# One product scales both heads of a query tile in the first attention, with the inverse sums in a PSUM bank

## The chip, the cores and the metric

The kernel runs on one core of a Trainium2 chip. The metric is device microseconds of one launch. The core has five queues of instructions that run side by side and wait for each other through semaphores: TensorE (PE) multiplies matrices into PSUM, VectorE (DVE) and ScalarE (ACT) work elementwise on SBUF and PSUM, GpSimd (POOL) works elementwise on SBUF, and SyncE (SP) issues DMAs. Within a queue the order is fixed when the program is built.

## The reference

Four batches, eight heads, 768 positions, 64 values a head. Attention sees the 96 positions behind a query (its own included) and the first 8 positions, with a bias that falls with distance. What comes out is the input of a mixture of four two-layer experts.

```python
scores = scale * np.matmul(q, k.transpose(0, 1, 3, 2)) + bias
scores = np.where(keep, scores, -1e9)
scores = scores - scores.max(-1, keepdims=True)
a = np.exp(scores)
a = a / (a.sum(-1, keepdims=True) + 1e-09)
x = np.matmul(a, v)                      # to (B*S, H*D) = (3072, 512)
for e in range(4):
    out += p[:, e:e+1] * (np.maximum(x @ w1[e], 0) @ w2[e])
```

## The kernel before, in words

**The first attention.** Batch 0 must have its attention output `x` before the experts have anything to multiply, so the launch begins with `attention_early`. It takes the heads in four pairs (0, 2, 1, 3), and each pair in six query tiles of 128 rows: 24 tiles in all. A tile's scores lie in windows of 256 columns per head (128 for the first tile of a pair). The local function `flow` drives a pipeline in which four tiles are in work at once. One call of `flow` does, in this order:

- `scores_early` for the newest tile and its neighbour (PE, in every second call);
- `softmax(one, two)`: for each head of tile *one*, DVE adds the bias and takes the minimum (`nmax`), and ACT takes the exponential and its row sum (`zsum`). Between them, DVE finishes tile *two*: it adds 1e-9 to `zsum`, takes the reciprocal, and scales the two heads of `pb` with one `tensor_scalar` each;
- `turn(three)`: PE transposes the scaled tile *three* into `pt`, and ACT copies it to `pT`;
- `weigh`, in every third call: PE multiplies the `pT` of three finished tiles by `v` into the bank `px` (20 matrix passes where the first tile of a pair is among them, 24 otherwise), and ACT copies 384 columns of `px` to `x`.

In a call with `weigh`, the three tiles were turned in earlier calls; tile *two* of that call, which DVE scales at the same time, is not among them.

So there are eight weighs: tiles 0 to 2 and tiles 3 to 5 of each pair. They are called the first to the eighth weigh below. The first falls into the call in which tile 4 of the pair is scaled, the second into the call in which tile 1 of the next pair is scaled, and so on. At the eighth no tile is left to scale.

**What sets the order.** While `Ordered.on` is set, each engine keeps the order in which the program is written. Waits are put in by the language's tile layer: an instruction that touches a tile waits for the last instructions of other engines that touched the same tile, whichever columns each of them used. All eight PSUM banks are taken in this stage: four by the scores, three by `pt`, one by `px`.

**Beside and behind it.** Between the calls of `flow`, POOL and SP prepare the first expert weights, and `first_sums` and `opening` start on the first expert as soon as half of `x` is there. Behind the attention PE works through the experts of batch 0, and the attention of the other batches is spread over the experts' work by `attention_chain`, which calls the same `softmax` and `weigh` with `early=False`.

The elementwise helper that records each instruction is line 43, so most rows of the profile carry L43; tiles are told apart by their names.

Of the kernel before, what the change touches and what calls it, by code (L numbers as in the profile page):

```python
# [9 lines left out]
F32 = mybir.dt.float32  # L10
# [3 lines left out]
AF = mybir.ActivationFunctionType  # L14
ALU = mybir.AluOpType
# [3 lines left out]
P = 128  # L19
# [167 lines left out]
def attn_moe_kernel(ctx: ExitStack, tc, q, k, v, n_global, n_local, domain_probs, w1, w2, out):  # L187
# [9 lines left out]
    HALF = S // 2  # L197
# [12 lines left out]
    ve, ac, po, sy, te = (Ordered(tc, e) for e in (nc.vector, nc.scalar, nc.gpsimd, nc.sync, nc.tensor))  # L210
# [173 lines left out]
    def windows(A, vt):  # L384

        vg = A.vg.tile([P, 2, NQT, D], F32, name="vg")
        sy.dma_start(vg[:NPREV], vt[NGLOB:])
        po.tensor_copy(vg[NPREV:], vt[:NGLOB, :, 0:1, :].to_broadcast([NGLOB, 2, NQT, D]))
        return vg
# [17 lines left out]
    def scores_early(A, t0, got):  # L407


        heads = [A.ps.tile([P, 2, 2 * P], F32, name=f"ps{j}") for j in range(2)]  # L410
        for t in (t0, t0 + 1):
            c0 = max(t - 1, 0) * PL + (0 if t == 0 else NGLOB)
            n = P if t == 0 else 2 * P
            for j in range(2):
                own = slice(j * D, (j + 1) * D)
                win = got["k"].rearrange("p t c -> p (t c)")[own, c0 : c0 + n]
                te.matmul(heads[j][:, t - t0, :n], got["q"][own, t, :], win, start=True, stop=True)
        return [[heads[j][:, i] for j in range(2)] for i in range(2)]

    def softmax(A, new, old):  # L420


        if old:
            pb, zsum = old["pb"], old["zsum"]
        if new:
            t, pr, ps = new["t"], new["pr"], new["ps"]
            cols = slice(0, P) if t == 0 else slice(0, 2 * P)
            bcol = slice(2 * P, 3 * P) if t == 0 else slice(0, 2 * P)
            new["pcol"] = pcol = slice(P, 2 * P) if t == 0 else slice(0, 2 * P)
            nmax = A.small.tile([P, 2], F32, name="nmax")  # L430
            new["zsum"] = A.small.tile([P, 2], F32, name="zsum")
            new["pb"] = A.pb.tile([P, 2, 2 * P], F32, name="pb")
        for j in range(2):
            if new:
                e = new["pb"][:, j, pcol]
                ve.tensor_tensor_reduce(
                    e, ps[j][:, cols], nbias[:, 2 * pr + j, bcol], 1.0, 3.0e38, ALU.add, ALU.min, nmax[:, j : j + 1]
                )
                ac.activation(
                    e, e, AF.Exp, bias=nmax[:, j : j + 1], scale=-1.0, accum_out=new["zsum"][:, j : j + 1]  # L440
                )
            if old:
                if j == 1:
                    ve.reciprocal(zsum, zsum)
                elif A.early:

                    old["spare"] = spare = A.small.tile([P, 3], F32, name="spare")
                    ve.tensor_scalar(zsum, zsum, 1e-9, None, op0=ALU.add, op1=ALU.add, accum_out=spare[:, 2:3])
                else:
                    ac.activation(zsum, zsum, AF.Copy, bias=1e-9)  # L450
        if old:
            for j in range(2):
                p = pb[:, j, old["pcol"]]
                if A.early:
                    ve.tensor_scalar(
                        p, p, zsum[:, j : j + 1], None, op0=ALU.mult, op1=ALU.add, accum_out=old["spare"][:, j : j + 1]
                    )
                else:
                    ac.activation(p, p, AF.Copy, scale=zsum[:, j : j + 1])

    def turn(A, tile_):

        t, pb = tile_["t"], tile_["pb"]
        pt = A.pt.tile([P, 2, 2, P], F32, name="pt")
        pT = A.pT.tile([P, 2, 2, P], F32, name="pT")
        w0 = 1 if t == 0 else 0
        for w in range(w0, 2):
            for j in range(2):
                te.transpose(pt[:, w, j, :], pb[:, j, w * P : (w + 1) * P], ident)
        ac.copy(pT[:, w0:], pt[:, w0:])  # L470
        tile_["pT"] = pT

    def weigh(A, three, x, b):

        px = A.px.tile([P, 512], F32, name=A.pxname)
        for i, tile_ in enumerate(three):
            t, pr, pT = tile_["t"], tile_["pr"], tile_["pT"]
            vt, vg = tile_["v"]["v"], tile_["v"]["vg"]
            for w in range(1 if t == 0 else 0, 2):
                for j in range(2):  # L480
                    vv = vt[:, j, t] if w == 1 else vg[:, j, t - 1]
                    te.matmul(
                        px[j * D : (j + 1) * D, i * P : (i + 1) * P],
                        vv,
                        pT[:, w, j, :],
                        start=(w == 1 if t == 0 else w == 0),
                        stop=(w == 1),
                    )
        cols = slice((t - TPH + 1) * P, (t + 1) * P)
        if x is not None:  # L490
            ac.copy(x[:, pr, cols], px[:, :HALF])
        else:
            piece = A.st.tile([P, HALF], F32, name="piece")
            ac.copy(piece, px[:, :HALF])
            ac.dma_start(xd[b][:, pr, cols], piece)
# [3 lines left out]
    def attention_early(A):  # L499

        b = 0
        x = xs[b] = xp.tile([P, NPAIR, S], F32, name="x")
        tiles, turned, ahead = [None] * 4, [], [None]

        def flow(new=None):

            one, two, three, four = tiles
            if new:
                if new["t"] % 2 == 0:
                    new["ps"], ahead[0] = scores_early(A, new["t"], gots[new["pr"]])  # L510
                else:
                    new["ps"] = ahead[0]
            if four:
                turned.append(four)
            softmax(A, one, two)
            if three:
                turn(A, three)
            if len(turned) == TPH:
                weigh(A, turned, x, b)
                turned.clear()  # L520
            tiles[:] = [new, one, two, three]

        def start(pr):

            nats[pr] = {n: next(load(A, src, b, pr, n)) for n, src in (("q", q), ("k", k), ("v", v))}

        def prepare_all(pr):

            nat, got = nats[pr], gots[pr]
            got["v"] = nat  # L530
            prepare_early(A, nat["q"], 0, "q", got)
            if pr:
                yield 1
            prepare_early(A, nat["k"], 0, "k", got)
            yield 1
            nat["vg"] = windows(A, nat["v"])
            prepare_early(A, nat["k"], 1, "k", got)
            yield 1
            prepare_early(A, nat["q"], 1, "q", got)
            yield 1  # L540

        nats, gots = {}, [{} for _ in range(NPAIR)]
        halves = [load(A, src, b, 0, n, 2) for n, src in (("q", q), ("k", k))]
        bias = biases(start_stack.enter_context(tc.tile_pool(name="setup", bufs=1)))
        next(bias)
        nats[0] = dict(zip(("q", "k"), (next(h) for h in halves)))
        for h in halves:
            next(h)
        nats[0]["v"] = next(load(A, v, b, 0, "v"))
        todo = [prepare_all(pr) for pr in PAIRS]  # L550
        next(bias)
        next(todo[0])
        start(PAIRS[1])
        for m, pr in enumerate(PAIRS):
            cur = gots[pr]
            for t in range(NQT):
                if t == 2 and m + 2 < NPAIR:
                    start(PAIRS[m + 2])
                flow({"t": t, "pr": pr, **cur})
                if (m, t) in BIASES:  # L560
                    next(bias)
                for _ in range(AHEAD[m][t]):
                    while todo and next(todo[0], 0) == 0:
                        todo.pop(0)
                yield
        while any(tiles):
            flow()
            yield
# [401 lines left out]
    with ExitStack() as start_stack:  # L970
        A = Pools(start_stack, "start", st=1, kd=2, qd=2, nat=2, natv=3, pb=4, ps=2, pt=3, px=1, early=True)
# [11 lines left out]
    op = main.enter_context(tc.tile_pool(name="op", bufs=1))  # L983
# [3 lines left out]
    A = Pools(  # L987
        att_stack, "att", st=1, kd=1, qd=2, nat=1, natv=1, pb=2, ps=2, pt=2, px=0, early=False, side="right"
    )
# [463 lines left out]
```

## Time and profile before

| what | value |
|---|---|
| median of 3 runs | 1165.45 us (1165.42 to 1165.84) |
| the profiled execution's own time | 1164.69 us |
| its span | 1162.9 us |
| PE busy | 1140.5 us, 98% |
| DVE busy | 853.2 us, 73% |
| ACT busy | 618.2 us, 53% |
| POOL busy | 606.6 us, 52% |

PE is the engine of the whole launch. The first 60 us, which hold the first attention, are another kind of stage: the four engines PE, ACT, DVE and POOL hand tiles to each other, and which of them is last changes on the way. The chain of waits (the profile's view of what ended last, followed back) and the timelines of single engines show that.

### The profile page before, as it was taken

To read this page: it belongs to the slowest core of one execution; us is meant where nothing else is said; L and a number is where in the kernel's file an instruction comes from. 1 tells how busy PE (TensorE), PEld (TensorE's weight loads), DVE (VectorE), ACT (ScalarE), POOL (GpSimd) and SP (SyncE) were. 2 spreads that over 40 slices of the span, in tenths; PEclk is the share of its full clock that TensorE was granted. 3 is DMA by queue.
4 is the path that set the end of the run, shared out by engine and by line. 5 is a ranking of instruction groups with operands and counts; after the bars stand their busy time and mean duration, and the time that the engine had idled before them with its cause. 6 is when DMAs were issued, how large, how long until landed. Compare 5 with 4: busy or idle time off the path is not lost.

```text
span 1162.9 us, 21146 instructions
## 1 busy us (share of the span) xinstructions
PE 1140.5 (98%) x7474; PEld 1062.6 (91%) x7474; DVE 853.2 (73%) x1944; ACT 618.2 (53%) x1597; POOL 606.6 (52%) x592
## 2 busy tenths in 40 slices
PE   7899999999999999999999999999999999999997
PEld 5678898989888989899998899999999999999997
DVE  7977776767767777776776777777777777777776
ACT  6854767777653665655565334444445444444443
POOL 5676645554343314222222327777778855555554
PEclk9999999999999999999999999999999999999999
DMA  9558798778775889978868668888887687777764
GB/s 185 149 172 290 268 294 258 269 253 255 247 261 206 282 269 286 282 234 279 257 196 288 207 215 304 306 302 300 284 314 281 240 303 239 249 247 247 245 232 131
DMA packets 181744, 294.32 MB, mean 253 GB/s; under 512 B 86400, under 2 KB 137088, under 8 KB 169344
## 3 DMA queue, kind: packets, MB, share of 16 engines
q1 hardware_dynamic: 177600, 286.61, 75.0%
q10 hardware_dynamic: 4032, 6.30, 1.5%
q8 instruction: 61, 1.00, 0.4%
q14 instruction: 51, 0.42, 0.1%
HBM read 207.93 MB, written 70.78 MB: 240 GB/s over the span
## 4 chain that ended last, share of the span: by engine, by line
PE 87%; DVE 5%; ACT 3%; POOL 2%; DMA 1%; issue 1%; DVEq 0%; ACTq 0%; POOLq 0%
PE pm L43 36%; PE pf L43 19%; PE X L43 11%; PE Y L43 9%; PE pt L43 7%; PE ps L43 4%; ACT pb L43 1%; DVE pb L43 1%; POOL w1s L43 1%; PE px L43 1%; DVE acc L43 1%; DVE xB L43 1%; DMA x_last<-piece 0%; DVE hA L43 0%; DVE pm L43 0%
## 5 line engine op out<-in xcount | busy, mean ns | idle before, releaser
L43 PE MATMUL pm<-w2s,h 128*128 128x512 f32 x1152 | 282.8, 395 | 3.6 <-DVE h L43 2.6
L43 PEld LDWEIGHTS pm<-w2s,h 128*128 128x128 f32 x1152 | 210.7, 188 | 46.5 <-DVE h L43 4.5
L43 ACT ACTIVATE hf<-pf 128x384 f32<-128x384 f32 x128 | 62.8, 491 | 248.3 <-DVE pf L43 247.1
L43 POOL TENSOR_TENSOR hS<-sf,hS 128x384 fp32r<-128x384 f32 x126 | 134.3, 1084 | 113.0 <-ACT hS L43 112.2
L43 DVE SCALAR_TENSOR_TENSOR acc<-pm,prob,acc 128x512 f32<-128x512 f32 x180 | 132.4, 748 | 54.5 <-PE pm L43 53.6
L43 POOL TENSOR_TENSOR sums<-raw 128x256 f32<-128x256 f32 x54 | 39.2, 745 | 211.8 <-DMA raw<-in_moe_w_dram 133.4
L43 PE MATMUL pm<-xT,w1s 128*128 128x384 f32 x744 | 147.9, 341 | 0.0
L43 PE MATMUL pf<-xT,w1s 128*128 128x384 f32 x768 | 146.5, 335 | 0.9 <-ACT hf L43 0.7
L43 PEld LDWEIGHTS pf<-xT,w1s 128*128 128x128 f32 x768 | 131.4, 188 | 1.7 <-ACT hf L43 1.2
L43 PEld LDWEIGHTS pm<-xT,w1s 128*128 128x128 f32 x744 | 128.0, 188 | 0.7 <-issue 0.7
L43 ACT ACTIVATE pb<-pb,nmax 128x256 f32<-128x256 f32 (+1 forms) x192 | 94.2, 498 | 58.1 <-DVE nmax L43 54.2
L43 DVE TENSOR_TENSOR hA<-hf,hA 128x384 fp32r<-128x384 f32 x94 | 84.6, 925 | 50.6 <-ACT hA L43 49.1
L43 PE MATMUL pm<-xB,w1s 128*128 128x384 f32 x574 | 116.8, 344 | 0.1
L43 PE MATMUL pf<-xB,w1s 128*128 128x384 f32 x576 | 110.7, 335 | 0.2 <-ACT hf L43 0.2
L43 PEld LDWEIGHTS pm<-xB,w1s 128*128 128x128 f32 x574 | 99.9, 188 | 5.5 <-issue 1.4
L43 ACT ACTIVATE h<-pm 128x384 fp32r<-128x384 f32 x128 | 62.0, 490 | 74.4 <-DVE pm L43 73.3
L43 PEld LDWEIGHTS pf<-xB,w1s 128*128 128x128 f32 x576 | 98.7, 188 | 0.6 <-ACT hf L43 0.4
L43 POOL TENSOR_TENSOR sf<-hf 128x384 f32<-128x384 f32 x63 | 70.3, 1116 | 43.6 <-ACT hf L43 43.6
L43 DVE CUSTOM_DVE_ANT_0 pb<-ps,nbias 128x256 f32<-128x256 f32 (+1 forms) x192 | 72.3, 395 | 5.8 <-PE ps L43 4.8
L43 DVE SCALAR_TENSOR_TENSOR h<-pm,h 128x384 fp32r<-128x384 f32 x128 | 69.5, 550 | 8.4 <-ACT h L43 6.8
L43 PE MATMUL Y<-w2b,hS 128*128 128x256 f32 x576 | 74.0, 282 | 0.0
L43 PE MATMUL X<-w2b,hS 128*128 128x256 f32 x576 | 73.9, 282 | 0.0
(159 smaller groups left out, 2183.5 us busy)
## 6 DMA issues: line engine op xcount, KB each, us to landing
w1s<-kept SPq DMA_DIRECT2D x47, 1792.0 KB, 8.2
w2b<-kept SPq DMA_DIRECT2D x224, 256.0 KB, 4.3
kept<-w1s SPq DMA_DIRECT2D x16, 1792.0 KB, 7.3
raw<-in_moe_w_dram SPq DMA_DIRECT2D x43, 512.0 KB, 4.7
kept<-w2s SPq DMA_DIRECT2D x16, 1024.0 KB, 6.9
w2s<-kept SPq DMA_DIRECT2D x16, 1024.0 KB, 5.5
qd<-qd SPq DMA_DIRECT2D x48, 192.0 KB, 3.2
v<-in_v_dram SPq DMA_DIRECT2D x16, 384.0 KB, 4.1
```

Source lines behind the costliest of these rows:

```text
L43: ins = fn(*args, **kwargs)
```

## The change

In the first attention alone, the reciprocal of `zsum` is written to four spare columns of the bank that `weigh` uses for `px` (two columns for tiles of even number, two for odd). One DVE `tensor_tensor` then multiplies both heads of the tile by these two numbers, broadcast along the columns. The bank `A.bank` is one tile for the whole stage, where before each `weigh` took a fresh tile from a pool with one buffer. The later attentions are as before.

```diff
             if old:
-                if j == 1:
+                if j == 1 and A.early:
+                    inverse = A.inverse[:, old["t"] % 2]
+                    ve.reciprocal(inverse, zsum)
+                elif j == 1:
                     ve.reciprocal(zsum, zsum)
                 elif A.early:
-                    old["spare"] = spare = A.small.tile([P, 3], F32, name="spare")
-                    ve.tensor_scalar(zsum, zsum, 1e-9, None, op0=ALU.add, op1=ALU.add, accum_out=spare[:, 2:3])
+                    spare = A.small.tile([P, 1], F32, name="spare")
+                    ve.tensor_scalar(zsum, zsum, 1e-9, None, op0=ALU.add, op1=ALU.add, accum_out=spare)
...
-        if old:
+        if old and A.early:
+            p = pb[:, :, old["pcol"]]
+            ve.tensor_tensor(p, inverse.unsqueeze(2).to_broadcast(list(p.shape)), p, op=ALU.mult)
+        elif old:
             for j in range(2):
                 p = pb[:, j, old["pcol"]]
-                if A.early:
-                    ve.tensor_scalar(
-                        p, p, zsum[:, j : j + 1], None, op0=ALU.mult, op1=ALU.add, accum_out=old["spare"][:, j : j + 1]
-                    )
-                else:
-                    ac.activation(p, p, AF.Copy, scale=zsum[:, j : j + 1])
+                ac.activation(p, p, AF.Copy, scale=zsum[:, j : j + 1])
...
     def weigh(A, three, x, b):
-        px = A.px.tile([P, 512], F32, name=A.pxname)
+        px = A.bank[:, :HALF] if A.early else A.px.tile([P, 512], F32, name=A.pxname)
...
     def attention_early(A):
         x = xs[b] = xp.tile([P, NPAIR, S], F32, name="x")
+        A.bank = A.px.tile([P, 512], F32, name="px")
+        A.inverse = A.bank[:, HALF : HALF + 4].rearrange("p (t j) -> p t j", j=2)
```

How the instructions stand, with the semaphores each waits for. First DVE at the second weigh: the end of the call in which tile 1 of the second pair is scaled, and the next call. `ISA pb,nmax<-ps,nbias` is the bias and minimum of one head, `zsum` the row sums. Before:

```order
L43 RECIPROCAL zsum<-zsum 128x2 [waits DVE_49]
L43 TENSOR_SCALAR pb,spare<-pb,zsum 128x256 [waits DVE_49]
L43 TENSOR_SCALAR pb,spare<-pb,zsum 128x256
L43 ISA pb,nmax<-ps_415,nbias 128x256 [waits PE_49]
L43 ISA nmax 128x1
L43 TENSOR_SCALAR zsum,spare<-zsum 128x2 [waits Activation_49]
L43 ISA pb,nmax<-ps_416,nbias 128x256
L43 ISA nmax 128x1
L43 RECIPROCAL zsum<-zsum 128x2 [waits DVE_49]
```

The same place now:

```order
L43 RECIPROCAL px<-zsum 128x2 [waits DVE_49]
L43 TENSOR_TENSOR pb<-px,pb 128x512 [waits DVE_49]
L43 ISA pb,nmax<-ps_409,nbias 128x256 [waits PE_49]
L43 ISA nmax 128x1
L43 TENSOR_SCALAR zsum,spare<-zsum 128x2 [waits Activation_49]
L43 ISA pb,nmax<-ps_410,nbias 128x256
L43 ISA nmax 128x1
L43 RECIPROCAL px<-zsum 128x2 [waits DVE_49,Activation_49]
L43 TENSOR_TENSOR pb<-px,pb 128x512 [waits DVE_49]
```

Two scalings have become one product, and the reciprocal of the call behind the weigh now also waits for ACT, whose last access to the bank is the copy from `px` to `x`. The same wait stands behind each of the first seven weighs.

PE at the same weigh: `pt<-ident,pb` are the transposes of tile *three*, `px<-pT` the products of the weigh. Before:

```order
L43 MATMUL pt<-ident,pb 128x128 [waits DVE_49,Activation_49]
L43 MATMUL pt<-ident,pb 128x128 [waits DVE_49]
L43 MATMUL px<-pT,vg 64x128 x2
L43 MATMUL px<-pT,v 64x128 x2
L43 MATMUL px<-pT,vg 64x128 x2
```

And now:

```order
L43 MATMUL pt<-ident,pb 128x128 [waits DVE_49,Activation_49]
L43 MATMUL pt<-ident,pb 128x128
L43 MATMUL px<-pT,vg 64x128 [waits DVE_49]
L43 MATMUL px<-pT,vg 64x128
L43 MATMUL px<-pT,v 64x128 x2
```

The order is the same, but the first product of the weigh now waits for DVE: for the product that scales tile *two* of the same call, the last DVE instruction before it in the program that read the bank. This wait stands at the first seven weighs as well.

SP in the first attention, at the loads of the last pair:

```order
+L1426 TENSOR_LOAD flag [waits Pool_49]
+L1426 ISA x2
 L43 DMA v<-in_v_dram 128x12x64 [waits DMAHW3_49,PE_49,Pool_49]
 L43 DMA vg<-v 96x768 [waits DMAHW5_49,DMAHW4_49]
 L43 DMA w1s<-in_moe_w_dram 128x4x256
-L43 DMA raw_490<-in_moe_w_dram 128x2x512 [waits DMAHW6_49]
-L1423 TENSOR_LOAD flag [waits Pool_49]
-L1423 ISA x2
+L43 DMA raw_481<-in_moe_w_dram 128x2x512 [waits DMAHW6_49]
```

The read of the flag for the general path stands four DMAs earlier. Behind the first attention no engine's order differs.

## Rows read from the trace of the kernel before

**Rows 1.** Stretches: start:end, length, busy us (instructions) by engine, PEclk, DMA, GB/s.
```profile
20.00:41.00 21.00, 20.70 (x204) 15.79 (x203) 19.30 (x124) 21.00 (x73) 11.96 (x16) 1.00 0.69 178
41.00:62.00 21.00, 16.66 (x147) 11.56 (x148) 17.39 (x93) 14.52 (x45) 13.23 (x15) 1.00 0.39 107
...
75.00:100.00 25.00, 25.00 (x134) 23.15 (x132) 18.52 (x33) 11.88 (x24) 22.79 (x22) 1.00 0.96 323
```

**Rows 2.** Chain that ended last, first 61 us: start, length, engine, tile, instructions.
```profile
36.60 1.22 ACT pb L43 x4
...
51.66 1.22 DVE pb L43 x5
...
59.98 0.49 ACT x L43
```

**Rows 3.** DVE timeline, second weigh: start, length, instruction, idle before it and releaser.
```profile
25.01 0.15 DVE L43 TENSOR_SCALAR_CACHE_REDUCE zsum<-zsum 128x2 f32<-128x2 f32 x1 [0.26 <-ACT pb L43]
...
25.44 0.16 DVE L43 RECIPROCAL zsum<-zsum 128x2 f32<-128x2 f32 x1
25.63 0.48 DVE L43 TENSOR_SCALAR_CACHE_REDUCE pb<-pb,zsum 128x256 f32<-128x256 f32 x1
...
26.04 0.47 DVE L43 TENSOR_SCALAR_CACHE_REDUCE pb<-pb,zsum 128x256 f32<-128x256 f32 x1
```

**Rows 4.** PE timeline, second weigh: its first and last products, then next transposes.
```profile
24.73 0.44 PE L43 MATMUL px<-pT,vg 128*64 128x128 f32 x4
...
25.87 0.39 PE L43 MATMUL px<-pT,v 128*64 128x128 f32 x4
...
27.73 0.66 PE L43 MATMUL pt<-ident,pb 128*128 128x128 f32 x4
```

**Rows 5.** ACT timeline, second weigh: copy of `px`, next copy of `pT`.
```profile
26.92 0.54 ACT L43 COPY x<-px 128x384 f32<-128x384 f32 x1
...
28.66 0.65 ACT L43 COPY pT<-pt 128x512 f32<-128x512 f32 x1
```

**Rows 6.** DVE timeline, reciprocals at the first, fifth, sixth and seventh weigh.
```profile
19.75 0.16 DVE L43 RECIPROCAL zsum<-zsum 128x2 f32<-128x2 f32 x1
...
43.28 0.15 DVE L43 RECIPROCAL zsum<-zsum 128x2 f32<-128x2 f32 x1
...
45.23 0.16 DVE L43 RECIPROCAL zsum<-zsum 128x2 f32<-128x2 f32 x1
...
49.70 0.16 DVE L43 RECIPROCAL zsum<-zsum 128x2 f32<-128x2 f32 x1
...
51.47 0.16 DVE L43 RECIPROCAL zsum<-zsum 128x2 f32<-128x2 f32 x1
...
55.00 0.16 DVE L43 RECIPROCAL zsum<-zsum 128x2 f32<-128x2 f32 x1
```

**Rows 7.** ACT timeline, copies of `px` at the first, fifth and sixth weigh.
```profile
21.49 0.50 ACT L43 COPY x<-px 128x384 f32<-128x384 f32 x1
...
44.49 0.47 ACT L43 COPY x<-px 128x384 f32<-128x384 f32 x1
...
50.71 0.47 ACT L43 COPY x<-px 128x384 f32<-128x384 f32 x1
```

**Rows 8.** PE timeline, after a wait, and the seventh weigh's first products.
```profile
48.43 0.50 PE L43 MATMUL pt<-ident,pb 128*128 128x128 f32 x2 [1.51 <-DVE pb L43]
...
54.85 0.44 PE L43 MATMUL px<-pT,v 128*64 128x128 f32 x4
```

**Rows 9.** DVE timeline, products of 384 and of 768 columns.
```profile
64.51 0.96 DVE L43 TENSOR_TENSOR xB<-x,xB 128x768 fp32r<-128x768 f32 x1 [1.34 <-ACT xB L43]
...
67.59 0.56 DVE L43 TENSOR_TENSOR u<-pm,u 128x384 f32<-128x384 f32 x1
```

**Rows 10.** One tile's instructions: `acc` from PSUM, ns of one as min/median/max.
```profile
L43 DVE SCALAR_TENSOR_TENSOR acc<-pm,prob,acc x11: 740/750/751, 94.9 to 119.0; 128x512 f32<-128x512 f32 x11
```

**Rows 11.** POOL timeline: the first instruction behind the attention.
```profile
65.29 1.86 POOL L43 TENSOR_TENSOR xT<-xB,xT 128x768 fp32r<-128x768 f32 x1 [9.94 <-ACT xT L43]
```

## The prediction

> **What bounds the kernel now.** I read the page's busy shares first, then the stretches, then the chain of waits, then the timelines of DVE, PE and ACT around each weigh. PE is busy 98% of the span, and behind the first attention it has no gap: 25.00 of the 25 us from 75 to 100 [rows 1]. So whatever makes `x` of batch 0 later moves everything behind it, unless a gap takes it in. The first attention has two stages. From 20 to 41 us ACT is busy 21.00 of 21 us while DVE has 19.30 [rows 1], the chain there runs through ACT's exponentials, and DVE waits for them before it adds 1e-9 to the sums [rows 2, 3]. From 41 to 57 us the chain runs through DVE's `pb`, and it ends with ACT's copy of the eighth weigh at 59.98 [rows 2]. In both stages the engines are interlocked within one or two microseconds, so a new wait among PE, ACT and DVE counts more than a shorter instruction on one of them.
>
> **What is removed.** Each of 24 tiles loses two scalings. At the second weigh they start at 25.63 and 26.04, 0.41 us apart [rows 3], so two take 0.82 us from start to start. The add of 1e-9 and the reciprocal stay.
>
> **What is added: the product.** No row shows a product of 512 columns with a broadcast operand. A product of 384 columns with one operand in PSUM takes 0.56 us, and one of 768 columns 0.96 us [rows 9]; the slope, 0.40 us for 384 columns, gives 0.56 + 0.13 = 0.69 us for 512. The nearest row of 512 columns from PSUM, with three operands, takes 0.75 us [rows 10]. I take 0.70 us. The ends are 0.56 us (the 384-column row itself, if the broadcast side came free) and 0.75 us. The next DVE instruction starts about 0.07 us before an instruction's end (0.48 long, 0.41 to the next start, [rows 3]), so the product takes 0.63 us from start to start, and a tile gains 0.82 - 0.63 = 0.19 us of DVE. The four first tiles of a pair, at half the width, gain about as much.
>
> The Trainium skill, in "VectorE: DVE Perf Modes", section "The perf-mode tier table", says that fp32 `tensor_scalar` in SBUF runs at two elements a cycle, and fp32 `tensor_tensor` at one. By that rule the two scalings should cost half of what the product costs, and the merger would lose DVE time. The trace does not agree for these scalings, which write an accumulator: 0.41 us for 256 columns is no faster per column than the 384-column product. By the rule the sum below would be about 2 us higher; I go by the rows.
>
> **What is added: two waits in a ring.** At the first seven weighs, PE's first `px` product waits for the product of tile *two* of the same call, and the next call's reciprocal waits for ACT's copy of `px`. Before, neither waited: at the second weigh PE began at 24.73, while the scalings ended at 26.51 [rows 3, 4]. Now the order is fixed: reciprocal, product, weigh on PE, copy on ACT, next reciprocal. From the start of the reciprocal: 0.19 to the product (25.44 to 25.63, [rows 3]), 0.70 product, 0.05 to PE (estimate: the small gaps that separate engines in the chain), the weigh, 0.04 to ACT. The weigh takes from 24.73 to 25.87 + 0.39, that is 1.53 us with six groups [rows 4]; one group is 0.22, so 1.31 with five groups. The copy thus starts 2.29 or 2.51 us after the reciprocal. What a wait costs beyond that is in no row of this place. Its lower end is 0; its upper end about 0.15 us each, from the nearest row: two transposes behind a wait of 1.51 us take 0.50 us, 0.25 each, where four without one take 0.66, 0.17 each [rows 4, 8]. I take 0, since the products of the seven weighs are of another shape than these transposes, and keep the other end for the range.
>
> *ACT's stage.* The reciprocal is pinned here to ACT's own exponential [rows 3], so each delay of the copy adds to ACT, which has no idle time.
> - First weigh: 19.75 + 2.29 = 22.04 against 21.49: 0.55 late [rows 6, 7].
> - Second: 25.44 + 2.51 = 27.95 against 26.92: 1.03 late [rows 3, 5].
> - Third and fourth repeat the pattern: 1.0 and 1.1.
> - Behind the second and the fourth, PE is late by more than ACT: 25.44 + 0.94 = 26.38 against 24.73, that is 1.65. What is queued behind its wait are the next transposes and scores; the transposes then end at 27.73 + 0.66 + 1.65 = 30.04, where ACT could copy at 28.66 + 1.03 = 29.69 [rows 4, 5]. That is 0.35 more, twice 0.7.
>
> Together 0.55 + 1.03 + 1.0 + 1.1 + 0.7 = 4.4 us.
>
> *DVE's stage.* Here the next reciprocal counts: copy start plus 0.47 for the copy [rows 7] and 0.03 to DVE.
> - Fifth weigh: 43.28 + 2.29 + 0.50 = 46.07 against 45.23: 0.84 [rows 6].
> - Sixth: 49.70 + 2.51 + 0.50 = 52.71 against 51.47: 1.24 [rows 6].
> - Seventh: nothing on DVE depends on the end, but PE does, whose order then is this weigh, two tiles' transposes, the opening product and the eighth weigh. It starts at 55.00 + 0.94 = 55.94 against 54.85: 1.09 [rows 6, 8].
>
> That is 3.2 us. Against it stand six tiles scaled outside these rings, 6 x 0.19 = 1.1 us, and some slack of DVE when the last place passes from ACT to it, about 0.5 us (an estimate: DVE idles 0.26 us for ACT in a call, [rows 3], and two calls pass).
>
> **The sum.** 4.4 + 3.2 - 1.1 - 0.5 = 6.0 us later. The 0.19 us of the five tiles before the first weigh I count at nothing, since the first reciprocal of a ring is pinned to ACT; if they did count, it would be 0.9 us less. SP's flag read is moved past `v`, `vg`, `w1s` and `raw`, in front of a `v` load that waits for PE anyway; and what POOL prepares from those loads has 9.94 us of idle time behind it [rows 11], so a later weight load of about two microseconds is covered; without that cover it would cost those two. The profiled execution took 1164.69 us, which gives 1170.7; the median of the runs shown is 0.76 higher, so 1171.4 us.
>
> The Trainium skill, in "PSUM — Partial Sum Buffer", section "PSUM bank collisions raise a hardware error", says that two engines must be kept apart by bank and partition quadrant, even in different columns. By it the waits are what sharing the bank requires, and the gain alone, 1 to 3 us off the time, could not be had with this placement. No run here shows a collision.
>
> **Rivals.**
> - *Absorbed.* The delay is there, but is partly taken in: DVE is ahead enough that the delay of ACT's stage does not add to that of its own, or short PE gaps behind 60 us close. For it: PE is busy only 16.66 of 21 us after 41 [rows 1]. Against it: the chain there is unbroken on DVE, and PE has no gap from 75 on. If half of ACT's 4.4 us went, 1171.4 - 2.2 = 1169.2; if all of it, 1167.0. Chance 0.20.
> - *The ring costs more.* PE starts slower after each wait (7 x 0.15 = 1.0), the product takes 0.75 (7 x 0.05 = 0.4), and PE, 20.70 of 21 us busy in ACT's stage [rows 1], does not catch up behind the first and the third weigh either (2 x 0.35 = 0.7): 2.1 more, 1173.5 us. Chance 0.13.
> - *Faster: the waits end early.* If DVE's shorter work let the product be finished before PE comes to each weigh, only the 0.19 us would count. In DVE's stage that is 8 tiles x 0.19 = 1.5, so 1165.45 - 1.5 = 1163.9 us. It decides from the point where DVE runs 1.7 us earlier against PE at a weigh (26.38 against 24.73). Against it: the reciprocal is pinned to ACT's exponential. Chance 0.03.
> - *No effect*: both sides cancel, within 0.2%. Chance 0.04.
>
> The forecast's own case, 5 to 7 us later, has 0.60. The range goes from 1167.6 (most of the absorbed case) to 1174.8 (the costlier ring with a margin for a second lag of PE). A change below 0.2%, some 2.3 us, is about what cannot be told from none here. Slower by more has 0.60 + 0.13 and most of the absorbed case, 0.15: 0.88. Within 0.2%: 0.05 of the absorbed case and the last rival: 0.09. Faster: 0.03.
>
> **What would show it.** Right: idle time of PE before `px`, released by DVE `pb`, at seven weighs; idle time of DVE before seven reciprocals, released by ACT's copy to `x`, about 1 us each; a 512-column product of 0.69 to 0.75 us; the copy of the eighth weigh at about 66 us instead of 59.98; ACT with idle time between 20 and 45 us; no other difference behind. The prediction is wrong if the last copy to `x` comes before 62.5 us, if these waits are short, or if the last copy is late and the end is not.

## The result, and the profile after

The change makes the kernel slower by 0.6%: 1171.68 us median of 7 runs (1169.01 to 1174.26) against 1165.26 us (1163.11 to 1165.84) for the kernel before, measured beside it. The ratio is 1.0060, 95% interval 1.0051 to 1.0070. The forecast was 1171.4 us, range 1167.6 to 1174.8. The profiled execution took 1172.23 us with a span of 1170.4.

Stretches of the span first, which answer to [rows 1]. The columns are the stretch, its length, busy time of PE, PE's weight load, DVE, ACT and POOL, the granted clock of PE, and the DMA share with GB/s:

```profile
20.00:41.00 21.00, 15.97 (x160) 12.37 (x159) 15.14 (x78) 18.59 (x62) 8.89 (x11) 1.00 0.60 144
41.00:62.00 21.00, 15.14 (x137) 11.27 (x133) 15.85 (x76) 14.33 (x48) 16.84 (x19) 0.92 0.52 142
51.00:54.00 3.00, 0.66 (x5) 0.21 (x3) 2.96 (x16) 1.92 (x6) 2.84 (x4) 1.00 0.00 0
54.00:58.00 4.00, 3.17 (x26) 2.84 (x28) 1.50 (x8) 1.28 (x6) 3.84 (x5) 0.61 0.61 164
75.00:100.00 25.00, 24.15 (x122) 21.18 (x121) 20.41 (x38) 13.68 (x26) 24.62 (x24) 1.00 0.86 275
```

ACT has lost its place as the full engine: it stands idle for 2.4 of the 21 us from 20 to 41, DVE for 5.9 and PE for 5.0. And one thing is new that no row of before had: from 54 to 58 us PE's granted clock is 0.61, that is, part of the stretch at 1.2 instead of 2.4 GHz.

Who waits for whom from 10 to 75 us (total, times, longest):

```profile
PE px L43 <- DVE pb L43: 9.5, 7, 2.0
DVE px L43 <- ACT x L43: 9.4, 7, 2.7
ACT x L43 <- PE px L43: 8.4, 8, 2.7
```

Both new waits stand at all seven weighs. At the second weigh the timeline of DVE (start, duration, engine, line, operation, in brackets the idle time before it and what ended it) answers to [rows 3]; the last reciprocal is that of the next call:

```profile
26.35 0.17 DVE L43 RECIPROCAL px<-zsum 128x2 f32<-128x2 f32 x1
26.56 0.69 DVE L43 TENSOR_TENSOR pb<-px,pb 128x512 f32<-128x512 f32 x1
...
29.39 0.17 DVE L43 RECIPROCAL px<-zsum 128x2 f32<-128x2 f32 x1 [1.12 <-ACT x L43]
```

PE at the second and the sixth weigh, for [rows 4]:

```profile
27.30 0.44 PE L43 MATMUL px<-pT,vg 128*64 128x128 f32 x4 [1.58 <-DVE pb L43]
...
52.42 0.41 PE L43 MATMUL pt<-ident,pb 128*128 128x128 f32 x2 [1.17 <-DVE pb L43]
54.83 0.69 PE L43 MATMUL px<-pT,vg 128*64 128x128 f32 x4 [2.00 <-DVE pb L43]
55.31 0.64 PE L43 MATMUL px<-pT,v 128*64 128x128 f32 x4
```

ACT's eight copies to `x`, and one to `pT` behind the second weigh, for [rows 5, 7]:

```profile
22.34 0.48 ACT L43 COPY x<-px 128x384 f32<-128x384 f32 x1 [0.45 <-PE px L43]
28.88 0.48 ACT L43 COPY x<-px 128x384 f32<-128x384 f32 x1 [0.89 <-PE px L43]
31.06 0.59 ACT L43 COPY pT<-pt 128x512 f32<-128x512 f32 x1 [0.24 <-PE pt L43]
35.77 0.48 ACT L43 COPY x<-px 128x384 f32<-128x384 f32 x1 [0.83 <-PE px L43]
42.31 0.48 ACT L43 COPY x<-px 128x384 f32<-128x384 f32 x1 [0.88 <-PE px L43]
49.06 0.48 ACT L43 COPY x<-px 128x384 f32<-128x384 f32 x1 [0.99 <-PE px L43]
57.70 0.48 ACT L43 COPY x<-px 128x384 f32<-128x384 f32 x1 [2.72 <-PE px L43]
64.06 0.48 ACT L43 COPY x<-px 128x384 f32<-128x384 f32 x1 [0.83 <-PE px L43]
67.83 0.48 ACT L43 COPY x<-px 128x384 f32<-128x384 f32 x1 [0.83 <-PE px L43]
```

Set against the same copies of before (21.49, 26.92, 32.41, 37.85, 44.49, 50.71, 56.22, 59.98) they are 0.85, 1.96, 3.36, 4.46, 4.57, 6.99, 7.84 and 7.85 us late. The lateness is built up at the weighs, almost nothing of it is given back, and the span of the profiled execution is 7.5 us longer (between the medians it is 6.4 us).

The chain of waits (start, length, engine and tile) gives the sixth and the eighth weigh, both with 24 passes:

```profile
54.83 2.83 PE px L43 x24
...
66.33 1.48 PE px L43 x24
67.83 0.49 ACT x L43
```

The sixth took 2.83 us at the lower clock, the eighth 1.48 at the full one; in the kernel before a weigh of 24 passes took 1.53 (second weigh, [rows 4]).

One caution for what follows: the first attention does not begin at the same distance from the span's start in every execution (the first copy to `x` lies at 22.34 in this profile and at 21.01 in a second one of the same kernel). So between kernels the time from the first copy to the last is compared as well: 38.49 us before, 45.49 after.

### The profile page after: what moved, and what is told of

It reads as the page before. It is cut to its first block, busy times and chain, and to the rows that moved or that the text cites. A ratio compares the mean times of both kernels' runs of the same rounds, so it can differ in the third digit from the quotient of the medians.

```text
span 1170.4 us, 21084 instructions
## 1 busy us (share of the span) xinstructions
PE 1141.1 (97%) x7474; PEld 1063.9 (91%) x7474; DVE 849.5 (73%) x1872; ACT 619.2 (53%) x1597; POOL 606.6 (52%) x592
## 4 chain that ended last, share of the span: by engine, by line
PE 90%; DVE 5%; ACT 2%; POOL 1%; issue 1%; DMA 0%; DVEq 0%; ACTq 0%
PE pm L43 39%; PE pf L43 19%; PE X L43 11%; PE Y L43 9%; PE pt L43 7%; PE ps L43 4%; PE px L43 1%; DVE pb L43 1%; ACT pb L43 1%; DVE hA L43 0%; POOL w1s L43 0%; DVE xB L43 0%; DVE acc L43 0%; POOL xB L43 0%; DVE u L43 0%
## 5 line engine op out<-in xcount | busy, mean ns | idle before, releaser
L43 PE MATMUL pm<-w2s,h 128*128 128x512 f32 x1152 | 282.9, 395 | 2.8 <-DVE h L43 1.8
L43 PEld LDWEIGHTS pm<-w2s,h 128*128 128x128 f32 x1152 | 210.7, 188 | 45.8 <-DVE h L43 3.6
L43 ACT ACTIVATE hf<-pf 128x384 f32<-128x384 f32 x128 | 62.8, 491 | 248.2 <-DVE pf L43 247.0
L43 POOL TENSOR_TENSOR hS<-sf,hS 128x384 fp32r<-128x384 f32 x126 | 134.3, 1084 | 113.2 <-ACT hS L43 112.5
L43 DVE SCALAR_TENSOR_TENSOR acc<-pm,prob,acc 128x512 f32<-128x512 f32 x180 | 132.5, 748 | 54.5 <-PE pm L43 53.8
L43 POOL TENSOR_TENSOR sums<-raw 128x256 f32<-128x256 f32 x54 | 38.8, 738 | 210.8 <-DMA raw<-in_moe_w_dram 158.0
L43 PE MATMUL pm<-xT,w1s 128*128 128x384 f32 x744 | 147.9, 341 | 0.0
L43 PE MATMUL pf<-xT,w1s 128*128 128x384 f32 x768 | 146.5, 335 | 0.9 <-ACT hf L43 0.7
L43 PEld LDWEIGHTS pf<-xT,w1s 128*128 128x128 f32 x768 | 131.3, 188 | 1.7 <-ACT hf L43 1.2
L43 PEld LDWEIGHTS pm<-xT,w1s 128*128 128x128 f32 x744 | 128.0, 188 | 0.7 <-issue 0.7
L43 ACT ACTIVATE pb<-pb,nmax 128x256 f32<-128x256 f32 (+1 forms) x192 | 93.1, 488 | 55.9 <-DVE nmax L43 54.0
L43 DVE TENSOR_TENSOR hA<-hf,hA 128x384 fp32r<-128x384 f32 x94 | 84.7, 927 | 50.5 <-ACT hA L43 49.1
L43 PE MATMUL pm<-xB,w1s 128*128 128x384 f32 x574 | 116.9, 344 | 0.1
L43 PE MATMUL pf<-xB,w1s 128*128 128x384 f32 x576 | 110.7, 335 | 0.2 <-ACT hf L43 0.2
L43 PEld LDWEIGHTS pm<-xB,w1s 128*128 128x128 f32 x574 | 99.9, 188 | 5.5 <-issue 1.4
L43 ACT ACTIVATE h<-pm 128x384 fp32r<-128x384 f32 x128 | 61.9, 490 | 73.6 <-DVE pm L43 72.5
L43 PEld LDWEIGHTS pf<-xB,w1s 128*128 128x128 f32 x576 | 98.7, 188 | 0.5 <-ACT hf L43 0.4
L43 POOL TENSOR_TENSOR sf<-hf 128x384 f32<-128x384 f32 x63 | 70.3, 1117 | 43.7 <-ACT hf L43 43.7
L43 DVE CUSTOM_DVE_ANT_0 pb<-ps,nbias 128x256 f32<-128x256 f32 (+1 forms) x192 | 72.4, 397 | 5.7 <-PE ps L43 4.4
L43 DVE SCALAR_TENSOR_TENSOR h<-pm,h 128x384 fp32r<-128x384 f32 x128 | 69.6, 552 | 7.6 <-ACT h L43 6.0
L43 PE MATMUL Y<-w2b,hS 128*128 128x256 f32 x576 | 74.0, 282 | 0.0
L43 PE MATMUL X<-w2b,hS 128*128 128x256 f32 x576 | 73.9, 282 | 0.0
```

The costliest lines, as they stand in the source:

```text
L43: ins = fn(*args, **kwargs)
```

## The experiments

The theory: the loss is the ring of waits that three engines form round the shared bank, and the product by itself gains. The rivals: the product is slow, the place in PSUM is, or the loss lies elsewhere. The first four kernels ran on one chip, the next three on another and the last three on a third, each set beside runs of the kernel before (1164.52, 1164.0 and 1164.84 us); the ratios are to those. The edits are shown shortened.

**1. The product without the shared bank.**

```diff
-inverse = A.inverse[:, old["t"] % 2]
+inverse = A.small.tile([P, 2], F32, name="inverse")
...
-px = A.bank[:, :HALF] if A.early else A.px.tile(...)
+px = A.px.tile([P, 512], F32, name=A.pxname)
```

> The product stays, but the inverse sums lie in a small SBUF tile and each weigh takes its own tile of the px pool as before, so neither new wait exists. Ring theory (the 6 us come from the two waits of the shared bank): the loss is gone, no idle time of PE before px released by DVE pb, and of the shorter DVE work about 8 x 0.19 us remain, so about 1163.8 us, 1163 to 1165.5. Rival, product theory (the 512-column product itself is slower than the two scalings in its place): still 2 to 6 us over before, 1167.5 or more. A second rival: the product now has both inputs in SBUF, and the difference xB of 384 columns took 1.31 instead of 0.55 us while POOL worked; if POOL holds it up in the same way from 41 to 57 us, 1166 to 1169 us without any wait for px.

Measured: 1166.8 us (11 runs), ratio 1.0016 [1.0007, 1.0025]. The waits of the ring are gone, and with them most of the loss, but not all. First, the product (columns: shortest/median/longest ns, first and last start) is not always 0.69 us; second, PE's clock fell here too, as a stretch shows:

```profile
L43 DVE TENSOR_TENSOR pb<-inverse,pb x24: 426/693/1720, 12.9 to 59.4; 128x512 f32<-128x512 f32 x20, 128x256 f32<-128x256 f32 x4
...
47.00:50.00 3.00, 0.67 (x4) 0.36 (x6) 2.97 (x11) 1.56 (x5) 2.84 (x4) 0.75 0.00 0
50.00:53.00 3.00, 3.00 (x26) 2.67 (x28) 2.93 (x16) 1.54 (x6) 2.92 (x4) 0.50 0.45 147
```

The second rival of the expectation held. The longest products, up to 1.72 us, lie where POOL is busy; DVE then holds PE up (for 2.47 us ahead of 49.34), PE does 0.67 us of work in 3 us, and its clock falls to half.

**2. The waits without the product.** The changed kernel with two `tensor_scalar` scalings that read the inverse from the shared bank.

```diff
-ve.tensor_tensor(p, inverse..., p, op=ALU.mult)
+for j in range(2):
+    p = pb[:, j, old["pcol"]]
+    ve.tensor_scalar(p, p, inverse[:, j : j + 1], None, op0=ALU.mult, ...)
```

> The inverse sums lie in the shared bank as in the changed kernel, but two scalings with an accumulator do the work of the one product, so the waits are there and the product is not. Ring theory: slower than the changed kernel, since the second scaling ends 0.19 us later after its reciprocal than the product does, in seven rings 1.3 us: about 1173 us, 1171.5 to 1174.5. Product theory: the loss is gone with the product, 1165 to 1166.5 us.

Measured: 1175.57 us (4 runs), ratio 1.0088 [1.0073, 1.0104]: the loss is there without the product, and larger than expected. The scalings make each turn of the ring longer, so that the next call's reciprocal waits longer than the 1.12 us above. In the profiled execution, the slowest of the four (1177.75 us), the clock also fell for longer than in the changed kernel:

```profile
29.41 0.17 DVE L43 RECIPROCAL px<-zsum 128x2 f32<-128x2 f32 x1 [1.32 <-ACT x L43]
...
41.00:62.00 21.00, 14.61 (x125) 10.85 (x125) 16.05 (x82) 12.30 (x41) 16.69 (x19) 0.87 0.52 142
62.00:75.00 13.00, 10.38 (x75) 7.66 (x72) 6.02 (x33) 6.12 (x16) 0.00 (x0) 0.82 0.00 1
```

**3. The same bank, the weigh ahead.** The weigh's products stand ahead of `softmax` in the call, the copy to `x` stays at its end.

```diff
+copy = None
+if len(turned) == TPH:
+    copy = weigh(A, turned, x, b)
 softmax(A, one, two)
...
+if copy:
+    copy()
```

> The changed kernel with the order inside a call moved: the weigh's products stand on PE ahead of the transposes of tile three and ahead of the softmax of the same call, while ACT's copy of px stays at the end of the call. Now px waits only for the product of the call before, the reciprocal of the same call waits for px, and the next reciprocal for the copy. Ring theory: PE and ACT no longer stand behind a product that is still to come; what is left is a reciprocal held up by about 0.5 us at seven weighs, mostly off the path in ACT's stage. About 1165 us, 1163.5 to 1167. Rival (any sharing of the bank costs the same, wherever the waits stand): 1170 or more.

Measured: 1163.88 us (11 runs) beside 1164.52 of before, ratio 0.9996 [0.9987, 1.0005], as expected. The bank, the product and the sharing are those of the changed kernel. Only the order differs, and the loss is gone (a gain is not shown): DVE's reciprocal now mostly waits for PE, for 0.9 us at most, instead of PE for the product and DVE for ACT's copy behind it.

```profile
DVE px L43 <- PE px L43: 4.1, 6, 0.9
...
25.41 0.17 DVE L43 RECIPROCAL px<-zsum 128x2 f32<-128x2 f32 x1 [0.69 <-PE px L43]
...
59.83 0.48 ACT L43 COPY x<-px 128x384 f32<-128x384 f32 x1 [0.83 <-PE px L43]
```

**4. Part of the ring alone.** The inverse lies in SBUF; behind each product a copy of two columns of `A.bank` makes the next instructions on that bank wait.

```diff
-inverse = A.inverse[:, old["t"] % 2]
+inverse = A.small.tile([P, 2], F32, name="inverse")
...
 ve.tensor_tensor(p, inverse..., p, op=ALU.mult)
+touched = A.small.tile([P, 2], F32, name="touched")
+ve.tensor_copy(touched, A.bank[:, HALF : HALF + 2])
```

> The inverse sums lie in SBUF, and behind each product DVE reads two columns of the px bank, which nothing uses. So PE still waits for DVE at seven weighs, by way of that read, but the second wait (for ACT's copy) stands behind the product instead of ahead of the reciprocal. Ring theory, with the first wait as the main cost: ACT's stage loses the same 4.4 us, the stage of DVE about 0.8 us less at each of two weighs, and 24 small reads add up to 1 us: 1169 to 1171.5 us. Rival (the wait ahead of the reciprocal is what costs, by holding up the product and the next transposes): 1165 to 1167.5 us.

Measured: 1173.13 us (4 runs), ratio 1.0069 [1.0054, 1.0085], above both expectations. The experiment did not cut the ring as meant: a mere read of two columns by DVE also waits for ACT's read of others (0.38 us), and what stands behind it on DVE then waits 0.85 us for scores that PE makes behind the late weigh. Below the stretch with the clock stand DVE behind the second weigh and one later product.

```profile
41.00:62.00 21.00, 16.20 (x122) 12.01 (x119) 16.34 (x70) 11.75 (x38) 19.03 (x19) 0.76 0.50 143
...
28.80 0.16 DVE L43 COPY touched<-px 128x2 f32<-128x2 f32 x1 [0.38 <-ACT x L43]
29.82 0.42 DVE L43 CUSTOM_DVE_ANT_0 pb<-ps,nbias 128x256 f32<-128x256 f32 x1 [0.85 <-PE ps L43]
...
44.43 0.81 DVE L43 TENSOR_TENSOR pb<-inverse,pb 128x512 f32<-128x512 f32 x1
```

So it is one more kernel with the ring, and it has the trouble of run 1 as well: its product has both inputs in SBUF, and from 44.43 to 56 us it takes between 0.80 and 1.22 us. How much of the 1173.13 us is either isn't shown. The profiled execution is the slowest of the four (1175.51 us, mean clock 0.993; the others took 1172.81 to 1173.40 at 0.997 or 0.998), so its 0.76 from 41 to 62 us doesn't stand for them.

**5. The inverse in a PSUM bank that ACT never touches.** It goes into two score columns of tile *one*, which DVE has just read; PE writes that bank again a call or more later.

```diff
-inverse = A.inverse[:, old["t"] % 2]
+inverse = (new or old)["ps"][0][:, 0:2]
...
-px = A.bank[:, :HALF] if A.early else A.px.tile(...)
+px = A.px.tile([P, 512], F32, name=A.pxname)
```

> The product stays and the inverse stays in PSUM, but in two dead columns of the score bank that DVE has just read, which PE and DVE alone use and PE writes again a call or more later; px is a fresh tile as before. Theory (the loss is the ring of three engines round one bank, not PSUM and not the product): no wait of PE px for DVE pb and none of DVE's reciprocal for ACT x; the product takes 0.69 us at every tile, also while POOL works, since one operand comes from PSUM; the copies to x start at or up to 0.5 us before those of the kernel before; 8 tiles x 0.19 = 1.5 us are gained in DVE's stage: 1163.0 us (1162 to 1165). First rival (any inverse in PSUM costs): 1168 to 1172. Second rival (the clock falls without the ring too, as in the run with the inverse in SBUF): 1165.5 to 1169.

Measured: 1162.06 us (11 runs) beside 1164.0 (17 runs), ratio 0.9981 [0.9972, 0.9990]. This is the version that beats both kernels. All products of 512 columns take 0.69 us, also while POOL works, PE's clock stays at 1.00, and from the first copy to the last it is 37.49 us instead of 38.49:

```profile
L43 DVE TENSOR_TENSOR pb<-ps,pb x24: 424/691/692, 12.9 to 54.0; 128x512 f32<-128x512 f32 x20, 128x256 f32<-128x256 f32 x4
...
41.00:62.00 21.00, 16.81 (x149) 11.99 (x148) 16.05 (x69) 14.49 (x44) 12.26 (x14) 1.00 0.34 102
...
20.43 0.51 ACT L43 COPY x<-px 128x384 f32<-128x384 f32 x1
57.92 0.48 ACT L43 COPY x<-px 128x384 f32<-128x384 f32 x1 [0.83 <-PE px L43]
```

Neither the product nor PSUM was the trouble: which engines use the bank, and when, was.

**6 to 10. PE's clock.** In these, PE repeats the transposes into the bank that it has just filled, so that it stands idle less: run 6 in the calls of the fifth to seventh weigh, run 7 the same in the kernel of run 2, run 8 in every call from behind the fourth weigh to the sixth, run 9 the same in the kernel before; run 10 is the changed kernel again.

```diff
+late = 4 <= weighs[0] < 6          # runs 8, 9
 if three:
-    turn(A, three)
+    turn(A, three, (5 if three["t"] == 0 else 3) if late else 1)
```

> The changed kernel, but the transposes of tile three are done three times over (8 transposes more) in the calls of the fifth, sixth and seventh weigh, where PE waits 1.3 to 2.0 us for DVE's product. Nothing waits for the second and third repetition but PE's own next product and ACT's copy to pT. Theory (the part of the loss beyond the ring is PE's clock, which falls after PE stood idle): the granted clock stays near 1.00 between 54 and 58 us, the sixth weigh takes about 1.5 us instead of 2.83, and the time is 1171.7 - 1.3 = 1170.4 us (1169 to 1171). Rival (the idle time of PE is not what lowers the clock, or the clock costs nothing at the end): as the changed kernel, 1171.7, or up to 1 us above it since the transposes delay ACT.

> The kernel with the waits of the shared bank but two scalings (1175.6 us when it ran, mean granted clock 0.994), with the same 8 transposes more in the calls of the fifth, sixth and seventh weigh. Theory (that kernel lost more than the changed one by PE's clock): 1171.5 to 1173.5 us, mean granted clock 0.997 or more, last copy to x at 67 to 70 us instead of 73.4. Rival (it lost more by the two scalings in the ring themselves): 1175 to 1176.

Measured: run 6 took 1173.64 us (1170.17 to 1174.15, 6 runs), ratio 1.0071 [1.0058, 1.0084], and not the 1170.4 that was expected if the clock stayed up. It did not stay up: it fell as before, though the wait ahead of the sixth weigh was half filled, so this run doesn't test what the fall costs:

```profile
54.91 0.69 PE L43 MATMUL px<-pT,vg 128*64 128x128 f32 x4 [1.12 <-DVE pb L43]
55.39 0.64 PE L43 MATMUL px<-pT,v 128*64 128x128 f32 x4
```

Run 7 took 1176.44 us (4 runs), ratio 1.0107 [1.0093, 1.0122], though in the profiled executions its mean clock was 0.997 instead of 0.994 and its last copy came at 70.17 instead of 73.42. With the same transposes repeated it is 2.8 us above run 6 (1176.44 - 1173.64), and what is left between them is the two scalings in the ring, as the rival said (its 1175 to 1176 us were a little low); from the first copy to the last it is 48.07 us against 45.48.

The times of runs 6 to 9 hold something else besides. From the last copy to the end of the span it is 1104.08 us in run 6 and 1102.57 in the changed kernel, though the copies themselves lie alike (45.48 and 45.49 us from first to last); 1104.83 in run 7 and 1102.58 in run 2; 1103.43 in run 8 and 1102.28 in run 10; 1103.89 in run 9 and 1102.92 in the kernel before. So in these profiles the kernels with repeated transposes lose 1.0 to 2.3 us behind the attention, where nothing is repeated. The cause is open; part of it in run 6 is a wait of 1.05 us of PE for DVE's `h` at 343.10, which the changed kernel doesn't have. The times of these runs alone don't show what the clock costs.

> The changed kernel, with the transposes of every tile done three times over from the call behind the fourth weigh to the call of the sixth (some 8 transposes, about 1 us of PE, more in each of six calls). In the run where only the calls of the weighs had them, PE still stood idle for 1.26 us before 52.51 and 1.12 us before 54.91, and the clock fell as before. Theory (PE's low activity over this stage lowers the clock): the granted clock is near 1.00 from 54 to 58 us, the sixth weigh takes about 1.5 us instead of 2.83, its copy to x starts at 56.3 to 57 instead of 57.7; the time is 0.5 to 1.5 us below that of the changed kernel, unless the transposes themselves hold PE up. Rival (something else lowers it): clock 0.5 again in the sixth weigh, and the time of the changed kernel or above.

> The kernel before with the same repeated transposes, for what they cost by themselves. If PE's idle time in DVE's stage takes them in: the time of the kernel before, 1164 to 1165.5 us, clock 1.00 throughout. If they hold PE up at the weighs: 1 to 2 us more.

> The changed kernel itself once more, on the same chip as the two others: 1170 to 1174 us. If the clock falls in some executions only, its times lie in groups, the higher ones at a lower mean clock.

Measured: 1172.04 us (5 runs), 1165.21 us (11 runs) and 1172.52 us (5 runs), beside 1164.84 of before; the ratios are 1.0061 [1.0047, 1.0075], 1.0000 [0.9991, 1.0009] and 1.0060 [1.0046, 1.0073]. In run 8 the sixth weigh ran at the full clock. The groups of the weigh, and a later stretch, before which the repeated transposes had ended and PE was idle for 0.94 us ahead of 60.05 and 0.93 ahead of 61.61:

```profile
55.35 0.44 PE L43 MATMUL px<-pT,vg 128*64 128x128 f32 x4 [0.93 <-DVE pb L43]
55.62 0.39 PE L43 MATMUL px<-pT,v 128*64 128x128 f32 x4
...
62.00:66.00 4.00, 4.00 (x26) 2.93 (x23) 0.86 (x2) 1.20 (x3) 0.00 (x0) 0.57 0.00 2
```

The sixth weigh of run 10, in the same set, had waited 2.00 us and ran at half:

```profile
53.81 0.70 PE L43 MATMUL px<-pT,vg 128*64 128x128 f32 x4 [2.00 <-DVE pb L43]
54.29 0.64 PE L43 MATMUL px<-pT,v 128*64 128x128 f32 x4
```

So the fall could be moved by filling PE's idle time: from the sixth weigh to the seventh. How much idle time brings it isn't shown, since in run 8 it came behind waits of 0.94 and 0.93 us, and at the second and the fourth weigh of the changed kernel it did not come behind 1.58 and 1.57. The theory held for the sixth weigh, not for the time, which is 0.5 us below run 10, within the spread of either. The fillers held up the fifth weigh by some 1.1 us (its copy starts 27.86 us behind the first instead of 26.71), and the clock fell later instead. In the kernel before (run 9) the same transposes cost nothing that can be told from none, and the clock stayed at 1.00.

What the falls cost is best seen between the two profiles of the changed kernel, run 10's and the one above. Up to the fifth copy they agree, 26.71 and 26.72 us behind the first. In run 10 the clock is down longer, at the seventh weigh too:

```profile
41.00:62.00 21.00, 14.91 (x113) 10.83 (x113) 15.14 (x69) 13.82 (x45) 16.91 (x19) 0.84 0.51 143
62.00:66.00 4.00, 3.24 (x25) 2.91 (x26) 1.31 (x5) 1.77 (x6) 0.00 (x0) 0.63 0.01 2
...
69.52 0.48 ACT L43 COPY x<-px 128x384 f32<-128x384 f32 x1 [0.83 <-PE px L43]
```

Its eighth copy comes 48.51 us behind the first instead of 45.49, 3.0 us later, and its span, counted from the first copy, ends 2.7 us later.

The times of one program go with its mean clock in the same way. The seven runs of the changed kernel took 1169.01 us at 0.999, 1171.23 to 1172.23 at 0.997 and 0.998, and 1173.50 and 1174.26 at 0.994; run 10 took 1170.90 and 1171.19 at 0.997 and 1172.52 to 1173.77 at 0.994 and 0.995; run 8 took 1171.49 to 1172.04 at 0.999 and 1.000, and 1173.70 and 1173.91 at 0.997. A mean clock doesn't say where the fall lies, though: the kernel before, whose clock in the profile is below 1.00 in the last 13 us alone (0.90), has runs of 0.997 to 0.999 too, and on the first chip those of 0.999 took 1163.14 to 1163.61 us and those of 0.997 1164.52 to 1166.05. So the fall costs 1.3 us at the sixth weigh alone, and some 3 us more where it lasts as long as in run 10; how much of the changed kernel's median it is stays open, since none of its profiles shows the ring at the full clock throughout.

## Why the prediction was right, point by point

- **The chain before**: read too simply. From 20 to 33.5 us the chain of waits runs through PE (at the second weigh `24.80 1.46 PE px L43 x24`), and only from there to 39.9 us through ACT's exponentials. It did no harm to the sum, since both engines were full there (20.70 and 21.00 of 21 us, [rows 1]).
- **The two waits**: right, at all seven weighs, in the places named. DVE's were longer than the "about 1 us each" of the signs, 9.4 us in all.
- **The product**: 0.70 us taken, 0.69 measured. The Trainium skill, "VectorE: DVE Perf Modes", section "The perf-mode tier table", gives fp32 `tensor_scalar` in SBUF twice the rate of `tensor_tensor`, by which the merger would lose DVE time; run 5, which has the product and no ring, is faster than the kernel before, so the rows decide. The prediction's "about 2 us higher" by that rule doesn't come out of its own terms: with scalings at half of 0.63 us, the six tiles would lose 1.9 us instead of gaining 1.1, so an estimate by that section of the Trainium skill is 3.0 us higher.
- **The ring's length**: from reciprocal to copy 2.29 us for a weigh of 20 passes and 2.51 for 24; measured 2.31 (20.03 to 22.34) and 2.53 (26.35 to 28.88). The wait itself cost nothing extra: at the full clock the first group behind it takes 0.44 us, as it did without a wait [rows 4].
- **ACT's stage**: 0.55 + 1.03 + 1.0 + 1.1 and one lag of 0.35 made 4.0 us by the fourth copy. Measured: 4.46, of which 0.28 is a later start of the stage. The lag behind the second weigh is 0.44: `pT` is 2.40 late (31.06 against 28.66), the copy to `x` ahead of it 1.96.
- **DVE's stage**: from the fourth copy to the eighth the sum had 0.35 + 3.2 - 1.1 - 0.5 = 1.95 us. Measured: 7.85 - 4.46 = 3.39. The spread was off: the fifth copy lost only 0.11, so that the gain and the slack are spent there. The sixth lost 2.42, and here a term is missing: 2.83 - 1.53 = 1.30 us, the weigh at half clock. Without it 2.09 us are left, near the sum.
- **SP's flag read**, put at nothing: borne out. The load of `w1s` is issued 2.59 us later (30.09 against 27.50), 1.96 of it the lateness of the stage, and POOL still waits 13.17 us for ACT before its first `xT`, so the loads have room.
- **The clock** is what the prediction missed. Everything behind a wait was priced at the full clock. The 1.30 us are most of the difference between 1170.7, worked out for the profiled execution, and its 1172.23; they are also most of the distance from the last copy's forecast, about 66 us, to the 67.83 measured. The step from there to the median then went the other way, 0.55 us down instead of 0.76 up, and that hid the missing term: the closeness of 0.3 us is partly luck. The mechanism, the ring of waits, is not luck: runs 1, 3 and 5 take the ring away and the loss goes (in run 1 most of it), and run 2 keeps it without the product and the loss stays.
- **The rivals.** Absorbed: no, 7.85 us at the last copy became 7.5 at the end. The ring costs more: the times came near it in some runs, but none of its terms appeared (no slow start behind a wait at the full clock, no product of 0.75 us, and the second and the fourth copy lost 1.11 and 1.10 us, without a further lag of 0.35). The waits end early: no, though run 3 shows the order in which they would. No effect: no, the interval of the ratio begins at 1.0051. The prediction also held that the gain could not be had with this placement: run 3 keeps the placement and loses nothing, but it gains nothing either (ratio 0.9996).

## What to carry to other kernels

Spare columns of a PSUM bank are not spare if other engines use the bank: ask who writes and reads it between, because the tile layer orders accesses to it by tile and not by column, and a short instruction then stands in a ring with a long one. Put a small operand where its only other users are already ordered against it (here the score bank: a ratio to the kernel before of 0.9981 against 1.0060), or change the order in which the program is written. And when a change makes TensorE wait in a stage where it is often idle already, price the work behind the waits at half clock too (here 2.83 instead of 1.53 us for a weigh).

## What the runs showed of the hardware that was not expected

- PE's granted clock fell to 0.50, 1.2 instead of 2.4 GHz, behind no idle stretch longer than 2.00 us in the changed kernel: it had idled 1.17 us ahead of 52.42 and 2.00 ahead of 54.83, with 0.41 us of work between (0.66 us of 3 from 51 to 54). In run 8 it fell behind two of 0.94 and 0.93. The kernel before, idle for 1.51 us ahead of its sixth weigh [rows 8], kept 1.00.
- The DVE product with both inputs in SBUF took up to 1.72 us instead of 0.69 while POOL worked (run 1); with the small input in PSUM it took 0.69 at every tile of 512 columns (run 5). The Trainium skill, "SBUF — State Buffer", section "Who interferes with whom", says that a DVE instruction with two SBUF inputs contends with a GpSimd instruction that reads SBUF, and that one with at most one, outside the modes that take two ports, does not. The two runs agree with it.
